# Attention followed by a bilinear feed-forward, on one core: the score products in another order, the side units of three batches placed anew, one product moved to GpSimd

## Chip, cores, metric

The kernel runs on one core of one Trainium2 chip. The metric is the device time of one execution in microseconds (us).

## The reference

Shapes: batch 8, heads 8, sequence 576, head size 64, 32 memory slots; feed-forward 512 to 1536 to 512.

```python
a = softmax(phi, axis=seq)                      # per memory slot
k_m = einsum('bhsm,bhsd->bhmd', a, k)           # 32 keys per head
v_m = einsum('bhsm,bhsd->bhmd', a, v)
attn = softmax(q @ k_m.T / sqrt(64))            # 576 x 32 per head
x = heads side by side of (attn @ v_m)          # 4608 x 512
out = ((x @ w_a) * (x @ w_b)) @ w_out
```

The kernel folds `v_m` into `w_a` and `w_b` ("vab"), so `x` is never made. For each batch it needs these *side units*:

- `exp`: exp of phi, on ACT.
- `kv`, `km`, `kvt`: sums of keys and values over the sequence (pkv), scaled copies of them (rep, VectorE), their transposes (pT, then kvT).
- `qt0` to `qt3`: transposes of q in 32x32 blocks (VectorE).
- `sc`, `e0`, `e1`: score products (pscore), exponentials E (ACT).
- `den`, `nr`: denominators (pD, then L = ln on ACT), R = exp(-L) on ACT, A = E x R, the *normalising product*.
- `v0` to `v2`, `x0` to `x2`: the fold (pva) and its copies from PSUM to vab, one on ACT and one on VectorE for each bank pair.

## The kernel before

Everything is placed by hand. The main loop emits *up* products of one batch (pa, pb: A times vab; ACT casts pa to a_sb, VectorE multiplies it with pb into ht) and after each step one slot of side units of the next batch; some products of the output stage (py, pv, px, with the ACT copy u and the output tile o_sb) fill up between them. GpSimd adds and subtracts parts of ht for that stage (h_sums) and issues the loads of later batches. In the slot strings below each word is one slot, `+` joins units and `-` leaves a slot empty.

```python
def scores(gs):
    ...
    for g in gs:                       # g: half of the heads
        t["pss", g] = [banks.take([P, NI, 32], F32, "pscore", hold=True) for _ in range(2)]
        for dh in range(2):            # the two halves of the contraction
            for z in range(2):
                for j in range(4):
                    r, hp = head(g, j)
                    row = 64 * r + 32 * z
                    nc.tensor.matmul(t["pss", g][z][0][32*j:32*j+32], kvT[row:row+32, ...], qTv[row:row+32, hp, ...],
                                     start=(dh == 0), stop=(dh == 1), tile_position=(row, 32 * j))
...
def normalise(g, hfs=slice(0, 2)):
    ...
    nc.scalar.activation(out=R, in_=L, func=AF.Exp, scale=-1.0)
    engine = nc.vector if b < 3 else nc.gpsimd
    engine.tensor_tensor(out=attn[b][:, g, sl], in0=E, in1=R, op=ALU.mult)
...
# inside the ups of batch 1 (second half): the units of batch 2
ups(half_steps(1, 1, 4), slots(2, "- kvt qt3 sc+e0+e1+den0 - nr0+den1+v0+x0a - - x0b+nr1 - v1+x1b x1a"))
# inside the ups of batch 2: the rest of batch 2, batch 3, and (with ') the start of batch 4
second = "v2_+x2a_+exp0 x2b_ exp1 - qt0+kv+km - qt1+qt2 kvt+qt3 sc+e0 - e1+v0+x0a ... - x2b+exp1' - qt0'+kv'+qt1' km' - qt2'+kvt'+qt3'"
```

The kernel hands out eight PSUM banks in turn: the next PSUM tile takes the bank that has been unused longest, so a matmul can wait for a bank that an ACT or VectorE copy has yet to read. In what follows a *tile* of TensorE is one 32x32 position; half `g` uses eight of the sixteen.

The softmax here doesn't subtract the row's maximum and nothing guards it: scores larger than these inputs give would overflow.

Of the kernel before, what the change touches and what calls it, by code (L numbers as in the profile page):

```python
# [18 lines left out]
def kernel(  # L19
# [11 lines left out]
    nc = tc.nc  # L31
# [60 lines left out]
    def load(b):  # L92
        load_phi(b)
        load_k(b)
        load_v(b)
        load_q(b)
# [84 lines left out]
    def head(g, j):  # L181

        jj = j ^ g
        return jj % 2, 2 * g + jj // 2

    def units(b):
# [91 lines left out]
        def scores(gs):  # L278
            if 0 in gs:
                t["E"] = mid.tile([P, 2, S], F16, name="E")  # L280
            if len(gs) > 1 and b > 2:
                work.settle()
            qTv = t["qT"].rearrange("p c (i s e) -> p c i e s", e=2, s=32)
            for g in gs:
                t["pss", g] = [banks.take([P, NI, 32], F32, "pscore", hold=True) for _ in range(2)]
                for dh in range(2):
                    for z in range(2):
                        for j in range(4):
                            r, hp = head(g, j)
                            row = 64 * r + 32 * z  # L290
                            nc.tensor.matmul(  # L291
                                t["pss", g][z][0][32 * j:32 * j + 32, :, :],
                                t["kvT"][row:row + 32, 2 * g + dh, M * j:M * j + M],
                                qTv[row:row + 32, hp, :, dh, :],
                                start=(dh == 0),
                                stop=(dh == 1),
                                tile_position=(row, 32 * j),
                            )
# [17 lines left out]
        def normalise(g, hfs=slice(0, 2)):  # L316
            if g == 0 and hfs.start == 0:
                attn[b] = mid.tile([P, 2, S], F16, name="A")
            sl = slice(HALF * hfs.start, HALF * hfs.stop)
            if hfs.start == 0:  # L320
                t["R", g] = small.tile([P, S], F16, name="R")
            nc.scalar.activation(out=t["R", g][:, sl], in_=t["L", g][:, sl], func=AF.Exp, scale=-1.0)  # L322
            engine = nc.vector if b < 3 else nc.gpsimd
            engine.tensor_tensor(out=attn[b][:, g, sl], in0=t["E"][:, g, sl], in1=t["R", g][:, sl], op=ALU.mult)  # L324

        def fold(lo, hi, zs):
# [27 lines left out]
        for z in range(2):  # L354
            u[f"exp{z}"] = one(exp_phi, z)
            u[f"ks{z}"] = one(sums, z, 0)
            u[f"kt{z}"] = one(transpose, z, 0)
            u[f"vs{z}"] = one(sums, z, 1)
            u[f"vt{z}"] = one(transpose, z, 1)
            u[f"s{z}"] = one(scores, (z,))  # L360
            u[f"e{z}"] = one(exp_scores, z)
            u[f"den{z}"] = one(denominators, z)
            u[f"nr{z}"] = one(normalise, z)
            for hf in range(2):
                u[f"nr{z}{hf}"] = one(normalise, z, slice(hf, hf + 1))
            for n in range(NCH):
                u[f"v{n}{'ab'[z]}"] = one(fold, 512 * n, 512 * (n + 1), (z,))
                u[f"x{n}{'ab'[z]}"] = one(take_fold, 512 * n, 512 * (n + 1), z)
            for n in range(2):
                u[f"hv{n}{'ab'[z]}"] = one(fold, 256 * n, 256 * (n + 1), (z,))  # L370
                u[f"hx{n}{'ab'[z]}"] = one(take_fold, 256 * n, 256 * (n + 1), z)
        for n in range(NCH):
            u[f"v{n}"] = one(fold, 512 * n, 512 * (n + 1), (0, 1))
        for x in range(4):
            u[f"qt{x}"] = one(q_transpose, x)
        u["sc"] = one(scores, (0, 1))
        u["kv"] = one(kv_sums)
        u["km"] = one(take_kv)
# [225 lines left out]
    def up(b, i, hfs):  # L604
        for hf in hfs:
            up_half(b, i, hf, 0)
        if len(hfs) > 1:
            yield
        for hf in hfs:
            up_half(b, i, hf, 1)  # L610
        yield

    def ups(steps, side=()):

        side = iter(side)
        for step in steps:
            for _ in up(*step):
                work.advance()
                next(side, us[step[0]]["-"])()
        for f in side:  # L620
            work.advance()
            f()
# [5 lines left out]
    def half_steps(b, hf, lo=0):  # L628

        return [(b, i, (hf,)) for i in range(lo, NFF)]  # L630
# [10 lines left out]
    def slots(b, names):  # L641

        def both(fs):
            return lambda: [f() for f in fs]
        def unit(n):
            if n == "fin":
                return lambda: work.pull(-work.done % NFF)
            if n == "L":
                return lambda: load(b + 2) if b + 2 < B else None
            if n[0] == "y":  # L650
                return lambda: some(int(n[1:]))
            if n[0] == "d" and n[1:].isdigit():
                return lambda: work.pull(int(n[1:]))
            return us[b + n.endswith("'") - n.endswith("_")][n.rstrip("'_")]

        return [both([unit(n) for n in x.split("+")]) for x in names.split()]
# [3 lines left out]
    def some(n):  # L660
        for _ in range(n):
            next(early, None)
# [24 lines left out]
    ups(steps(1, 0, 4), slots(1, "- hv1a+hx1a hv1b+hx1b+y1 - v1a+x1a y3+v1b x1b y3"))  # L687
    ups(half_steps(1, 0, 4), slots(1, "- v2a+x2a+v2b+x2b+qt0' - - qt1'+exp0'+qt2' exp1' - kv'+km'+y9"))
    work.plan(S + HALF, 10)
    ups(half_steps(1, 1, 4), slots(2, "- kvt qt3 sc+e0+e1+den0 - nr0+den1+v0+x0a - - x0b+nr1 - v1+x1b x1a"))  # L690
    second = "v2_+x2a_+exp0 x2b_ exp1 - qt0+kv+km - qt1+qt2 kvt+qt3 sc+e0 - e1+v0+x0a den0+x0b v1+x1a nr0+L x1b+exp0' den1 - nr1+v2+x2a - x2b+exp1' - qt0'+kv'+qt1' km' - qt2'+kvt'+qt3'"
    every = "- sc+e0 e1 den0 v0+x0a+x0b - - nr0+exp0' - - v1+x1a qt0' x1b+den1 exp1' - v2+x2a+x2b nr1+qt1' kv'+km' qt2' - qt3' - kvt'+L -"
    last = "sc+e0 - e1 - v0+x0b - x0a den1 - - den0 v1+x1b x1a+nr0 - - - - nr1+v2+x2a - - - - - x2b"
    for b in range(2, B):
# [37 lines left out]
```

## Time and profile before

| | before |
|---|---|
| median | 246.36 us (246.25 to 246.43) |
| TensorE busy | 233.6 us, 95% of a span of 244.6 us |
| VectorE, ACT, GpSimd busy | 69%, 64%, 63% |
| TensorE's three waits between 60 and 110 us | A 1.0, E 0.5, rep 0.4 us |
| idle TensorE from 105 to 203 us | none |

In the timelines each line is one merged run of alike instructions: start, length, engine, line, operation and, in brackets, how long the engine stood idle before it and what ended that. The prediction below shows the page's first line, the stages and the timelines. TensorE's waits of over 0.15 us between 60 and 203 us all stand where batches 2 and 4 are prepared. Its longest one, and the next up product after batch 2's last fold, from its timeline:

```profile
74.20 0.28 PE L591 MATMUL pa<-A,vab 128*128 128x288 f16 x1 [1.04 <-DVE A L324]
...
75.73 0.42 PE L591 MATMUL pa<-A,vab 128*128 128x288 f16 x2
```

### The profile page before, as it was taken

The numbers are of one execution on the slowest core, as the hardware profiler recorded it, in microseconds if no ns is written. First come the engines' busy times: TensorE is split into PE (matmuls) and PEld (weight loads), VectorE is DVE, ScalarE is ACT, GpSimd is POOL, SyncE is SP. The second block draws the span as 40 slices with busy tenths as digits, with TensorE's granted clock in tenths as the row PEclk, the third lists the DMA queues.
The fourth block names the chain that finished last, engine by engine and source line by source line (L and its number), as shares of the span: only waits on it lengthen the run. The fifth ranks groups of instructions, "written<-read, shape, count | busy, mean of one in ns | idle before, by whom it ended". The sixth has DMA issues, their size and how long they took to land.

```text
span 244.6 us, 7659 instructions
## 1 busy us (share of the span) xinstructions
PE 233.6 (95%) x3043; PEld 167.7 (69%) x3043; DVE 167.7 (69%) x403; ACT 157.2 (64%) x406; POOL 153.1 (63%) x128
## 2 busy tenths in 40 slices
PE   7979998999998999999999999999999999999993
PEld 2545654456666857767788777877787878888882
DVE  3536773568869868876994659865996576756642
ACT  2355761679697489578856768577856867565330
POOL 8722263499898029892899759892849177937001
PEclk9999999999999999999999999999999999999999
DMA  6999999999989704973159832696120403032154
GB/s 198 210 207 207 211 251 208 255 225 280 221 199 207 156 3 114 240 125 86 34 143 211 180 86 46 163 206 151 29 62 3 88 0 87 3 88 60 43 128 117
DMA packets 25044, 33.82 MB, mean 138 GB/s; under 512 B 1936, under 2 KB 19472, under 8 KB 25008
## 3 DMA queue, kind: packets, MB, share of 16 engines
q0 software_dynamic: 18288, 22.84, 50.3%
q1 hardware_dynamic: 6208, 9.70, 16.0%
q10 hardware_dynamic: 512, 0.79, 0.9%
q8 instruction: 24, 0.39, 0.7%
q14 instruction: 12, 0.10, 0.1%
HBM read 42.47 MB, written 9.44 MB: 212 GB/s over the span
## 4 chain that ended last, share of the span: by engine, by line
PE 77%; DMA 16%; DVE 3%; ACT 1%; issue 1%; POOL 0%; DVEq 0%
PE pa L591 18%; PE py L463 17%; PE pb L591 17%; PE pv L463 8%; DMA wo_sb<-in_moe_w_out_dram 7%; DMA wa_sb<-in_moe_w_a_dram 6%; PE pva L336 5%; PE px L463 4%; PE po L388 3%; DMA ht<-in_k_dram 2%; PE pkv L212 2%; PE pD L313 2%; PE pscore L291 1%; PE pT L241 1%; DVE A L324 1%
## 5 line engine op out<-in xcount | busy, mean ns | idle before, releaser
L602 DVE TENSOR_TENSOR ht<-a_sb,pb 128x288 f16<-128x288 f16 x168 | 73.1, 448 | 38.2 <-ACT a_sb L599 29.2
L591 PEld LDWEIGHTS <-vab 128*128 128x128 f16 x768 | 71.6, 98 | 28.2 <-issue 10.4
L599 ACT CAST a_sb<-pa 128x288 f16<-128x288 f32 x168 | 66.4, 406 | 28.0 <-PE pa L591 26.1
L591 PE MATMUL pa<-A,vab 128*128 128x288 f16 x384 | 75.8, 287 | 1.4 <-DVE A L324 1.0
L591 PE MATMUL pb<-A,vab 128*128 128x288 f16 x384 | 75.0, 286 | 0.3 <-ACT vab L348 0.3
L445 POOL TENSOR_TENSOR h_sums<-ht 128x768 f16<-128x768 f16 x28 | 45.9, 1641 | 37.8 <-DVE ht L602 37.3
L463 PEld LDWEIGHTS <-h_sums 128*128 128x128 f16 x384 | 37.4, 98 | 6.9 <-issue 0.4
L348 DVE CAST vab<-pva 128x512 f16<-128x512 f32 (+1 forms) x50 | 32.4, 663 | 3.3 <-PE pva L336 2.6
L348 ACT CAST vab<-pva 128x512 f16<-128x512 f32 (+1 forms) x50 | 27.9, 577 | 9.4 <-PE pva L336 9.3
L463 PEld LDWEIGHTS <-ht 128*128 128x128 f16 x288 | 28.2, 98 | 5.6 <-issue 0.4
L463 PE MATMUL py<-w_sums,h_sums 128*128 128x256 f16 x192 | 30.3, 272 | 0.0
L445 POOL TENSOR_TENSOR h_sums<-h_sums,ht 128x768 f16<-128x768 f16 x14 | 23.1, 1650 | 0.9
L445 POOL TENSOR_TENSOR h_sums<-ht,h_sums 128x768 f16<-128x768 f16 x14 | 23.0, 1643 | 1.0
L304 ACT ACTIVATE E<-pscore 128x288 f16<-128x288 f32 x32 | 11.4, 416 | 13.0 <-PE pscore L291 12.9
L324 POOL TENSOR_TENSOR A<-E,R 128x576 f16<-128x576 f16 x10 | 12.8, 1278 | 7.0 <-ACT R L322 6.8
L463 PE MATMUL py<-wo_sb,ht 128*128 128x256 f16 x96 | 16.0, 273 | 0.0
L463 PE MATMUL pv<-w_sums,h_sums 128*128 128x256 f16 x96 | 16.0, 272 | 0.0
L203 DVE STREAM_TRANSPOSE qT<-q_sb 128x288 f32<-128x288 f32 x32 | 14.3, 461 | 2.3 <-DMA q_sb<-in_q_dram 2.3
L470 ACT ACTIVATE u<-py 128x256 f32<-128x256 f32 x32 | 12.4, 388 | 5.2 <-PE py L463 4.9
L463 PE MATMUL py<-w_sums,ht 128*128 128x256 f16 x96 | 15.5, 272 | 0.1
L463 PE MATMUL px<-wo_sb,ht 128*128 128x256 f16 x96 | 15.4, 273 | 0.0
L314 ACT ACTIVATE L<-pD 128x288 f32<-128x288 f32 x32 | 11.5, 418 | 5.0 <-PE pD L313 4.7
(65 smaller groups left out, 274.0 us busy)
## 6 DMA issues: line engine op xcount, KB each, us to landing
out_dram<-o_sb SPq DMA_DIRECT2D x68, 128.0 KB, 2.4
kv_sb<-in_v_dram POOLq DMA_DIRECT2D x7, 576.0 KB, 10.4
phi_sb<-in_phi_dram POOLq DMA_DIRECT2D x7, 576.0 KB, 5.1
kv_sb<-in_k_dram POOLq DMA_DIRECT2D x7, 576.0 KB, 8.5
q_sb<-in_q_dram POOLq DMA_DIRECT2D x6, 576.0 KB, 13.1
wa_sb<-in_moe_w_a_dram POOLq DMA_DIRECT2D x3, 512.0 KB, 15.0
wb_sb<-in_moe_w_b_dram POOLq DMA_DIRECT2D x3, 512.0 KB, 16.2
wo_sb<-in_moe_w_out_dram POOLq DMA_DIRECT2D x3, 512.0 KB, 17.5
```

Source lines behind the costliest of these rows:

```text
L203: nc.vector.transpose(out=t["qT"][:, hp, :].bitcast(F32), in_=qs[b][:, hp, :].bitcast(F32))
L304: nc.scalar.activation(out=Ev[:, g, :, z, :], in_=pss, func=AF.Exp, scale=1.0 / (8.0 * CS))
L314: nc.scalar.activation(out=t["L", g][:, sl], in_=pD, func=AF.Ln)
L324: engine.tensor_tensor(out=attn[b][:, g, sl], in0=t["E"][:, g, sl], in1=t["R", g][:, sl], op=ALU.mult)
L336: nc.tensor.matmul(t["pva", lo, z][g][0][32 * j:32 * j + 32, 0:hi - lo], t["kvT"][64 * r:64 * r + 64, 4 + g, M * j:M * j + M], w_sbs[z][64 ...
L348: engine_copy(out=vabs[b][z][:, g, lo:hi], in_=pva[:, 0:hi - lo])
L445: engine.tensor_tensor(out=out, in0=in0, in1=in1, op=op)
L463: nc.tensor.matmul(po, lhs[:, i], rhs[:, i], start=first and i == 0, stop=i == KH - 1, skip_group_check=not first)
L470: nc.scalar.mul(out=x, in_=po, mul=scale)
L591: nc.tensor.matmul(ps, vabs[b][x][:, g, P * i:P * (i + 1)], attn[b][:, g, HALF * hf:HALF * (hf + 1)], start=(g == 0), stop=(g == 1))
L599: nc.scalar.copy(out=a_sbs[b, i, hf], in_=ps)
L602: nc.vector.tensor_tensor(out=ht[:, i, t0:t0 + HALF], in0=a_sbs.pop((b, i, hf)), in1=ps, op=ALU.mult)
```

## The change

Its intent: let sixteen different tiles follow one another in the score products, and take away TensorE's waits for E, A (batch 2) and rep (batch 4).

```diff
-            for g in gs:   # (banks taken here, unchanged)
-                for dh in range(2):
-                    for z in range(2):
+            for dh in range(2):
+                for z in range(2):
+                    for g in gs:
                         for j in range(4):
...
-            engine = nc.vector if b < 3 else nc.gpsimd
+            engine = nc.vector if b < 2 else nc.gpsimd
...
-    ... slots(2, "- kvt qt3 sc+e0+e1+den0 - nr0+den1+v0+x0a - - x0b+nr1 - v1+x1b x1a"))
+    ... slots(2, "- kvt qt3 sc+e0+e1 - den0+den1 nr0+nr1 v0+x0a x0b - v1+x1b x1a"))
-    second = "... - qt0+kv+km - qt1+qt2 kvt+qt3 sc+e0 - e1+v0+x0a ... - qt0'+kv'+qt1' km' - qt2'+kvt'+qt3'"
+    second = "... - kv+km qt0 qt1 kvt qt2+qt3 sc+e0 e1+v0+x0a ... - kv'+km' qt0'+qt1' - qt2'+kvt'+qt3'"
```

More of the change, by code (lines that the diff above doesn't have):

```diff
@@ L689 @@
     work.plan(S + HALF, 10)
-    ups(half_steps(1, 1, 4), slots(2, "- kvt qt3 sc+e0+e1+den0 - nr0+den1+v0+x0a - - x0b+nr1 - v1+x1b x1a"))
-    second = "v2_+x2a_+exp0 x2b_ exp1 - qt0+kv+km - qt1+qt2 kvt+qt3 sc+e0 - e1+v0+x0a den0+x0b v1+x1a nr0+L x1b+exp0' den1 - nr1+v2+x2a - x2b+exp1' - qt0'+kv'+qt1' km' - qt2'+kvt'+qt3'"
+    ups(half_steps(1, 1, 4), slots(2, "- kvt qt3 sc+e0+e1 - den0+den1 nr0+nr1 v0+x0a x0b - v1+x1b x1a"))
+    second = "v2_+x2a_+exp0 x2b_ exp1 - kv+km qt0 qt1 kvt qt2+qt3 sc+e0 e1+v0+x0a den0+x0b v1+x1a nr0+L x1b+exp0' den1 - nr1+v2+x2a - x2b+exp1' - kv'+km' qt0'+qt1' - qt2'+kvt'+qt3'"
     every = "- sc+e0 e1 den0 v0+x0a+x0b - - nr0+exp0' - - v1+x1a qt0' x1b+den1 exp1' - v2+x2a+x2b nr1+qt1' kv'+km' qt2' - qt3' - kvt'+L -"
```

## The prediction

> **What bounds the kernel now.** I read the page first, then busy time by stage, then what TensorE waits for, then the timelines around those waits.
>
> ```profile
> PE 233.6 (95%) x3043; PEld 167.7 (69%) x3043; DVE 167.7 (69%) x403; ACT 157.2 (64%) x406; POOL 153.1 (63%) x128
> ```
>
> TensorE has 95% of the span, no other engine over 69%. Busy time by stage (columns: stretch, length, then busy us of PE, PEld, DVE, ACT, POOL, with clock and DMA) says where the missing 5% lies.
>
> ```profile
> 65.98:76.00 10.02, 8.43 (x125) 5.03 (x125) 7.24 (x15) 8.77 (x25) 9.84 (x9) 1.00 0.97 203
> 76.00:98.00 22.00, 21.92 (x311) 16.15 (x309) 17.69 (x44) 17.36 (x46) 10.52 (x9) 1.00 0.54 110
> 98.00:105.20 7.20, 6.84 (x151) 4.87 (x150) 6.28 (x19) 3.71 (x11) 6.31 (x5) 1.00 1.18 235
> 105.20:203.00 97.80, 97.80 (x1253) 75.19 (x1250) 72.29 (x171) 72.21 (x191) 69.70 (x49) 1.00 0.48 101
> ```
>
> From 105 to 203 us TensorE is never idle: there only less TensorE work can help. Before that, two stretches lose 1.59 and 0.36 us; these hold batches 2 and 4's side units, and TensorE's waits from 60 to 110 us are just three:
>
> ```profile
> PE pa L591 <- DVE A L324: 1.0, 1, 1.0
> PE pD L313 <- ACT E L304: 0.5, 1, 0.5
> PE pT L241 <- DVE rep L232: 0.4, 1, 0.4
> ```
>
> The change aims at all three. Timelines of batch 2 (start us, duration us, engine, line, instruction) show the first wait's origin:
>
> ```profile
> 69.64 0.46 DVE L324 TENSOR_TENSOR A<-E,R 128x576 f16<-128x576 f16 x1
> ...
> 72.70 1.45 DVE L324 TENSOR_TENSOR A<-E,R 128x576 f16<-128x576 f16 x1
> ```
> ```profile
> 72.17 1.65 POOL L445 TENSOR_TENSOR h_sums<-ht 128x768 f16<-128x768 f16 x1
> ```
>
> The same product took 0.46 us while GpSimd issued transfers, and 1.45 us when it started inside a GpSimd sum.
>
> **What the Trainium skill says.** "SBUF — State Buffer", section "Who interferes with whom": a VectorE instruction with two SBUF inputs and a GpSimd one that reads SBUF exclude each other; the later is blocked whole. The trace agrees: the sum ended at 72.17 + 1.65 = 73.82, and the product ended at 74.15. "GPSIMD Engine Reference", section 4.1: two-input elementwise work is about twice as slow on GpSimd. Here it is 1.278 us (group of ten) against 0.46, 2.8 times. "TensorEngine Tiling (Array Packing)", Key Properties: different tiles work in parallel, and a change of tiling mode drains the array. The trace agrees with both: going from 128x128 to 32x32 costs 94 ns over the ordinary spacing (last start before a score block 159.459 us, 256 columns of about 109 ns, first score start 159.662). "TensorE: Matmul & The Clock Gate", Part 3, The mechanism: matmuls start in strict program order. The trace disagrees: in batch 5's score block the second visit to the first eight tiles starts at 159.803, after the first visit to the other eight (159.715), although the program has it earlier.
>
> **The change part by part.**
>
> 1. *Score order.* One block is 32 matmuls of 32x32x288. A tile's second visit starts 0.141 us after its first (159.662 to 159.803), starts within a group are about 3.3 ns apart. Before: eight tiles, the same eight, the other eight twice; since the chip already lets the other eight overtake, the last start was 159.879, 0.217 us after the first. After: 16 x 3.3 = 53 ns for the first visits, and the last second visit starts at 0.141 + 0.053 = 0.194 us. That is 23 ns per block, not half of it. What follows is fixed: last start to the next matmul takes 0.215 us (159.879 to 160.094). Batches 0 and 1 make scores for one half alone, so nothing moves there. Batches 2 and 4 wait for other data (below). Left are batches 3, 5, 6, 7: 4 x 23 = **0.1 us**.
>
> 2. *Batch 2: product to GpSimd, the denominators two slots later, both normalisations together.* TensorE's stalls here: the wait for E (0.55 idle), the wait for A (1.04), and bank waits. I worked ACT through, for it runs without a gap from 66.47 to 73.91. Pitches from this trace: E 0.295 us, L 0.29, R 0.59, a_sb 0.35, vab 0.47, u 0.28. The first E starts some 0.15 later than before (66.62), as it now shares the wait for the last q transpose (matmul start 66.243) with the rest. Then 4 E, 2 a_sb, 4 L, a_sb, u put R at 70.3 and 70.9, ending at 71.0 and 71.6. GpSimd has ended its fourth sum at 69.2, so A is made 71.04 to 72.3 and 72.3 to **73.5**; before it was ready at 74.15. The other chain to the same matmul is a_sb (to 71.9), ht on VectorE (to 72.3), the copy of the first fold (to 72.95), which frees the bank that the v1 fold waits for; TensorE then starts batch 2's up products at 73.62 and the half that needs the second A at 73.74. It was 74.197. The v2 fold, held by the v1 copies (TensorE's 0.2 us there becomes about the same), passes at 75.33 where the next up product was at 75.735. The stalls for E and A, 1.6 us together, so give back only **0.4 us**, because ACT has the same work to do between them: TensorE arrives early and waits for banks instead. GpSimd's 2 x 1.28 = 2.56 us delay the loads of batch 4 and the next sums; before, the sums ended at 78.97 and the first was used at 83.7; after, they start near 76.5, the first ends at 78.2, the last at 83.1, needed near 89. Hidden.
>
> 3. *Batch 3's units.* The score block moves one slot later, its exponentials' second half and the v0 fold come right after. The fold's second half finds its bank held by an a_sb that ACT takes between the exponentials: about 0.3 us of wait, as now (the block v0 took 87.298 to 88.172, 0.874, where an undisturbed one takes 0.557), plus 0.1 at the next up product and 0.07 at a bank of the k-v sums. **-0.15 us**.
>
> 4. *Batch 4's units.* km now comes before the q transposes, so rep is done before 101.8 and the 0.8 us that the six pT transposes lose (0.36 idle, the rest hidden in weight loads) goes. But VectorE is full here:
>
> ```profile
> 102.10 0.74 DVE L232 TENSOR_SCALAR rep<-pkv,rphi 128x256 f16<-128x256 f32 x2
> 102.77 0.44 DVE L602 TENSOR_TENSOR ht<-a_sb,pb 128x288 f16<-128x288 f16 x1
> 103.13 0.47 DVE L203 STREAM_TRANSPOSE qT<-q_sb 128x288 f32<-128x288 f32 x1
> 103.52 0.52 DVE L242 COPY kvT<-pT 128x768 f16<-128x768 f16 x1
> 103.96 0.46 DVE L203 STREAM_TRANSPOSE qT<-q_sb 128x288 f32<-128x288 f32 x1
> 104.34 0.41 DVE L602 TENSOR_TENSOR ht<-a_sb,pb 128x288 f16<-128x288 f16 x1
> ```
>
> It runs from 99.17 to 105.5 without a gap, and the score block's last eight first visits began at 104.812, just after that last ht (104.76) freed their bank. The built program of the changed kernel has the same set of VectorE work ahead of that ht, in another order. So the score block waits where pT waited: **0 us** of its own.
>
> Sum: 0.1 + 0.4 - 0.15 + 0 = 0.35 us. TensorE's full stretch to 203 us carries the gain to the end, where the last waits (0.2 us) follow ht of the last batch and move along. 246.36 - 0.35 = **246.0 us**.
>
> **The rivals.** *All stalls vanish.* If the waits for E, A and rep go and nothing takes their place, 0.55 + 1.04 + 0.8 is 2.4 us, and with the score order some 2.5: 243.9. For it speaks that TensorE is the bound and these are its only waits; against it the gapless ACT and VectorE stretches. *The tile order halves a score block.* Two visits of 0.12 us streaming would be 0.24 instead of four; at 0.22 us for each of six blocks, 1.3 us: 244.7. Against it, the overtaking seen in the trace. *GpSimd comes in the way.* Two products of 1.28 us in a row end later than the VectorE one would: if R comes 0.7 us later than I have it (one more wait for a bank ahead of an L), A is ready at 74.2 and the gain of part 2 is gone; with batch 3's loss the time is 246.4 or 246.5. *No change*: every stall only moves, 246.3.
>
> **Range and chances.** Part 2 decides: it is between 0 and about 1.2 us (1.6 less what remains of bank waits), with 0.4 most likely; part 4 between 0 and 0.5, if VectorE's order lets its last ht finish earlier; part 3 between -0.3 and +0.2. Together 245.2 to 246.6. A change of over 2% would be 4.9 us, twice what all stalls hold, and for a slowdown nothing of that size is in sight: 1% each way.
>
> **What would show it.** In the changed profile: score blocks in batches 5 to 7 have the last start about 0.19 us after the first and the next up product about 23 ns earlier than 0.43; A on GpSimd twelve times at 1.28, the second of batch 2 ending near 73.5; batch 2's first up product near 73.6, waiting for a bank or for A; the pT transposes of batch 4 without a wait, but a score block near 104.3 that stands until ht; from 105 to 203 a full TensorE. I am wrong if ACT has idle time between 66.6 and 72 us (then part 2 is smaller), if the E and A waits go and no bank wait follows (then it is larger), or if the q transposes of batch 3 or 4 wait for late loads.

## The result

The changed kernel takes 245.59 us (245.41 to 245.71, four runs), the kernel before 246.31 us (246.20 to 246.43) in the same rounds. The ratio is 0.997, interval 0.9953 to 0.9988. It is a real gain of about 0.7 us, far within 2%.

The page of the changed kernel, and its busy time by stage, with the columns as before:

```profile
PE 234.6 (96%) x3043; PEld 168.1 (69%) x3043; DVE 166.2 (68%) x401; ACT 157.2 (64%) x406; POOL 155.6 (64%) x130
```
```profile
65.98:76.00 10.02, 9.38 (x130) 5.68 (x130) 5.89 (x13) 9.26 (x25) 8.17 (x8) 1.00 0.46 93
76.00:98.00 22.00, 21.92 (x310) 16.18 (x308) 17.70 (x43) 17.38 (x46) 15.05 (x13) 1.00 0.80 163
98.00:105.20 7.20, 6.97 (x151) 5.09 (x149) 6.16 (x18) 3.76 (x11) 6.47 (x5) 1.00 1.18 232
105.20:203.00 97.80, 97.80 (x1251) 75.12 (x1250) 72.25 (x171) 72.24 (x191) 69.78 (x50) 1.00 0.48 101
```

In batch 2's stretch TensorE is busy 0.95 us longer, but gets through only five more matmuls, so "busy" overstates the gain. A matmul's record is equally long whether the next one is held or not (those of the v1 fold take 0.37 to 0.39 us, and without a hold the next starts 3 ns after), and only idle time beyond its end counts as waiting. A hold of up to that length hides behind the record. ACT is now busy 9.26 of 10.02 us. What TensorE waits for between 60 and 110 us:

```profile
PE pD L314 <- DVE ht L603: 0.2, 1, 0.2
PE pva L337 <- DVE vab L349: 0.2, 1, 0.2
```

All three waits of before are gone; two bank waits stand in their place. The timeline of TensorE in batch 2 shows them, and one that the list does not name, inside the group at 71.90 (its first matmul starts at 71.897 and its second only at 72.385, which leaves 0.12 us of idle time, too little for the list):

```profile
68.86 0.28 PE L314 MATMUL pD<-E,ones 128*128 128x288 f16 x1 [0.20 <-DVE ht L603]
...
71.90 0.90 PE L337 MATMUL pva<-wa_sb,kvT 64*32 64x512 f16 x8
72.41 0.39 PE L337 MATMUL pva<-wb_sb,kvT 64*32 64x512 f16 x1
72.99 0.41 PE L337 MATMUL pva<-wb_sb,kvT 64*32 64x512 f16 x7 [0.19 <-DVE vab L349]
73.33 0.39 PE L464 MATMUL pv<-wo_sb,h_sums 128*128 128x256 f16 x2
73.55 0.41 PE L592 MATMUL pa<-A,vab 128*128 128x288 f16 x2
...
75.16 0.42 PE L592 MATMUL pa<-A,vab 128*128 128x288 f16 x2
```

The v1 fold (71.90 to 73.33, 1.43 us) takes 0.87 us longer than the v0 fold just before it (70.49 to 71.05, 0.56 us): it waits for banks that ht and the fold copies have yet to read. The second A (GpSimd's timeline) is ready at 71.07 + 2.51 = 73.58, just before TensorE comes to the half that needs it (73.676):

```profile
71.07 2.51 POOL L325 TENSOR_TENSOR A<-E,R 128x576 f16<-128x576 f16 x2 [1.81 <-ACT R L323]
```

**Reading parts inside a trace.** The start-up, up to batch 2's score block, is the same program in all thirteen kernels, yet the block starts at 65.52 to 66.54 us in their profiles. So I take that start as zero and compare where the same matmul stands later: the up product after batch 2's v2 fold (before: 75.735 - 65.982 = 9.75 us), the one after batch 3's v1 fold (24.58), the one after batch 4's scores (39.20), and the last matmul of the third px group from the end (163.82). The table gives the difference to the kernel before, negative when earlier, one profile each.

| run | after v2 fold, batch 2 | after v1 fold, batch 3 | after scores, batch 4 | near the end |
|---|---|---|---|---|
| changed kernel | -0.61 | -0.52 | -0.58 | -0.62 |
| order_only | +0.19 | +0.20 | +0.20 | +0.12 |
| old_order | -0.82 | -0.73 | -0.79 | -0.76 |
| product_vector | -0.53 | -0.44 | -0.50 | -0.58 |
| old_slots2 | -0.12 | -0.03 | -0.09 | -0.13 |
| old_slots34 | -0.60 | -0.60 | -0.59 | -0.64 |
| q_early | -0.61 | -0.52 | -1.30 | -1.35 |
| casts_vector | -1.05 | -0.97 | -1.03 | -1.10 |
| best | -0.23 | -0.15 | -0.93 | -1.01 |
| best2 | -1.07 | -0.99 | -1.77 | -1.85 |
| best3 | -1.60 | -1.52 | -2.30 | -2.38 |
| best4 | -0.42 | -0.33 | -1.11 | -1.19 |

What a stage gains stays to the end, because TensorE is full from 105 to 203 us. How far one profile can be trusted, the rows show themselves: the changed kernel, q_early and old_slots34 are the same program up to the first point and stand at -0.607, -0.608 and -0.603 there.

### The profile page after: what moved, and what is told of

Same layout as the page of the kernel before. It is cut to its first block, busy times and chain, and to the rows that moved or that the text cites. A ratio compares the mean times of both kernels' runs of the same rounds, so it can differ in the third digit from the quotient of the medians. Undisturbed runs are those within 1.5% of the kernel's fastest.

```text
span 244.0 us, 7661 instructions
## 1 busy us (share of the span) xinstructions
PE 234.6 (96%) x3043; PEld 168.1 (69%) x3043; DVE 166.2 (68%) x401; ACT 157.2 (64%) x406; POOL 155.6 (64%) x130
## 4 chain that ended last, share of the span: by engine, by line
PE 76%; DMA 16%; DVE 3%; ACT 2%; issue 1%; POOL 0%; DVEq 0%
PE pa L592 17%; PE py L464 17%; PE pb L592 16%; PE pv L464 8%; DMA wo_sb<-in_moe_w_out_dram 7%; DMA wa_sb<-in_moe_w_a_dram 6%; PE pva L337 5%; PE px L464 4%; PE po L389 3%; DMA ht<-in_k_dram 2%; PE pkv L212 2%; PE pscore L292 1%; PE pD L314 1%; PE pT L241 1%; ACT E L305 1%
## 5 line engine op out<-in xcount | busy, mean ns | idle before, releaser
L325 POOL TENSOR_TENSOR A<-E,R 128x576 f16<-128x576 f16 x12 | 15.3, 1278 | 8.8 <-ACT R L323 8.6
L194 ACT ACTIVATE exp_sb<-phi_sb 128x576 f16<-128x576 f32 x16 | 11.0, 698 | 5.3 <-DMA phi_sb<-in_phi_dram 5.3
```

The lines of the kernel that those rows point to most:

```text
L194: nc.scalar.activation(out=t["exp"][:, 2 * z:2 * z + 2, :, :], in_=phis[b][:, 2 * z:2 * z + 2, :].rearrange("p c (i m) -> p c i m", m=M), ...
L325: engine.tensor_tensor(out=attn[b][:, g, sl], in0=t["E"][:, g, sl], in1=t["R", g][:, sl], op=ALU.mult)
```

## The experiments

My theory: the order saves only nanoseconds, batch 2 gains by its placement as far as ACT's chain and the banks allow, batch 4 gains almost nothing because VectorE's queue is full. The rivals: the order is the gain; the engine of the product is the gain; a removed wait is worth its length. All runs below gave correct results; each kernel had four to six timed runs, against 11 or 12 of the kernel before. The changed kernel was not run again; the others are compared with its four runs above and with its trace.

### order_only: the order alone

```diff
 # kernel before
-            for g in gs:
-                for dh in range(2):
-                    for z in range(2):
+            for dh in range(2):
+                for z in range(2):
+                    for g in gs:
```

> The kernel before with the new order of the score products and nothing else. Theory (the chip lets other tiles overtake, so the order saves only the 23 ns between the last starts of batches 3, 5, 6, 7; batches 2 and 4 wait for data): 0.07 to 0.12 us faster than before, about 246.2. Rival (the order halves each of six score blocks): 1.3 us faster, about 245.0. In the trace: last score start 0.19 us after the first, against 0.217.

Measured: 246.39 us, ratio 1.0004 (0.9992 to 1.0016). The rival's 1.3 us is excluded. The trace shows that my sum was wrong in sign: TensorE loses 0.19 us in batch 2 and wins back 0.08 us by the end. ACT's timelines show why, first the kernel before, then this one (the score block starts at 65.98 and 66.03):

```profile
66.47 1.32 ACT L304 ACTIVATE E<-pscore 128x288 f16<-128x288 f32 x4
```
```profile
66.73 1.01 ACT L305 ACTIVATE E<-pscore 128x288 f16<-128x288 f32 x3 [0.32 <-PE pscore L292]
```

In batch 2 the last q transpose comes after the block has begun. Before, half 0 did not need it and its E could start 0.49 us after the block's start (66.47 - 65.98). In the new order a matmul that needs it is the seventh of 32, so that none of the four score banks is complete before it in the program, and E starts 0.70 us after (66.73 - 66.03). In the undisturbed blocks the gain is as small as I had it: in batch 6 the single records give 0.190 us from first to last start in the changed kernel, 0.217 before.

```profile
159.66 0.50 PE L291 MATMUL pscore<-qT,kvT 32*32 32x288 f16 x32
160.09 0.42 PE L591 MATMUL pa<-A,vab 128*128 128x288 f16 x2
```
```profile
159.08 0.47 PE L292 MATMUL pscore<-qT,kvT 32*32 32x288 f16 x32
159.49 0.42 PE L592 MATMUL pa<-A,vab 128*128 128x288 f16 x2
```

From block to next product: 0.43 before (first fence), 0.41 in the changed kernel (second).

### old_order: everything but the order

```diff
 # changed kernel
-            for dh in range(2):
-                for z in range(2):
-                    for g in gs:
+            for g in gs:
+                for dh in range(2):
+                    for z in range(2):
```

> The changed kernel with the score products in the order of before. Theory: 0.05 to 0.12 us slower than the changed kernel, about 245.7. Rival (the order carries the gain): the whole 0.7 us goes, 246.3.

Measured: 245.46 us, ratio 0.9967 (0.9955 to 0.9979), against 0.997 for the changed kernel; the times cannot tell the two apart. The traces can: without the new order TensorE leaves batch 2 another 0.21 us earlier (-0.82 against -0.61) and is 0.13 us ahead near the end. My expectation had the sign wrong, and the rival is out: the gain stays without the new order. The new order is a small loss in this kernel.

### product_vector: batch 2's product back on VectorE

```diff
 # changed kernel
-            engine = nc.vector if b < 2 else nc.gpsimd
+            engine = nc.vector if b < 3 else nc.gpsimd
```

> The changed kernel with batch 2's normalising products back on VectorE, units placed as in the changed kernel. Theory (what counts is that the products no longer start inside a GpSimd sum, and that ACT's chain sets R; with the new placement R is ready near 70.9 and 71.5 us while GpSimd only issues loads, until about 72.2): both products take about 0.46 us, and the time is within 0.2 us of the changed kernel. Rival (GpSimd is what takes the product out of the way; on VectorE it takes 1.45 us and holds TensorE as before): 0.6 to 0.9 us slower than the changed kernel.

Measured: 245.63 us, ratio 0.9978 (0.9966 to 0.999), within the 0.2 us expected. (The profile is of the longest run, 246.37 us, whose score block starts 0.5 us later than the changed kernel's.) TensorE leaves batch 2 at -0.53 instead of -0.61. VectorE's and GpSimd's timelines of this run:

```profile
71.55 1.02 DVE L325 TENSOR_TENSOR A<-E,R 128x576 f16<-128x576 f16 x2 [0.40 <-ACT R L323]
72.48 0.45 DVE L603 TENSOR_TENSOR ht<-a_sb,pb 128x288 f16<-128x288 f16 x1
```
```profile
71.97 0.75 POOL L90 DMA_DIRECT2D q_sb<-in_q_dram  x1
73.02 1.64 POOL L446 TENSOR_TENSOR h_sums<-ht 128x768 f16<-128x768 f16 x1 [0.30 <-DVE ht L603]
```

Two products take 1.02 us together, not 1.45 us for one, since GpSimd only issues loads until 72.7. So GpSimd is not what saves the product here: the new placement moves it out of the sum's way on either engine. What GpSimd adds is some 0.08 us, which fits ht: with the products ahead of it in VectorE's queue it starts 5.94 us after the block's start (72.48 - 66.54) instead of 5.87 (71.88 - 66.01).

### old_slots2: batch 2's units as before, product on GpSimd

```diff
 # changed kernel
-"- kvt qt3 sc+e0+e1 - den0+den1 nr0+nr1 v0+x0a x0b - v1+x1b x1a"
+"- kvt qt3 sc+e0+e1+den0 - nr0+den1+v0+x0a - - x0b+nr1 - v1+x1b x1a"
```

> The changed kernel with batch 2's units placed as before (denominators at once after the scores, normalisations apart), product on GpSimd. Theory: the 0.55 us wait for E is back, the second R ends near 72.7 again, GpSimd makes the second A to about 74.0, so TensorE's first up product of batch 2 is about 0.3 us later than in the changed kernel: 245.9. Rival (the engine of the product is all that counts): same as the changed kernel, 245.6. Rival (the placement is all): 246.2 to 246.3.

Measured: 246.05 us, ratio 0.9991 (0.9978 to 1.0004), between the rivals, and 0.46 us above the changed kernel where I had expected 0.3. TensorE's waits between 60 and 110 us in this run:

```profile
PE pa L592 <- POOL A L325: 0.9, 1, 0.9
PE pD L314 <- ACT E L305: 0.7, 1, 0.7
```

The wait for E is back, and longer than before the change (0.7 against 0.5), which fits the new order's 0.2. With order_only at +0.19 and this run at -0.12, moving the product alone is worth 0.30 us where units stand as before. Going from this run to the changed kernel, -0.12 to -0.61, placement is worth 0.49 us. The trace shows where the 0.30 us come from: the half that needs the second A starts 8.295 us after the block's start, in order_only 8.401, and the v2 fold is no longer held for 0.19 us by VectorE's copies, ahead of which the product had stood.

With product_vector, all four combinations have been run (all with the new order): placement is worth 0.72 us with the product on VectorE (+0.19 to -0.53). It is a bundle, though: denominators later, normalisations together, folds after both. No run separates these moves.

### old_slots34: the units of batches 3 and 4 as before

```diff
 # changed kernel
-second = "... - kv+km qt0 qt1 kvt qt2+qt3 sc+e0 e1+v0+x0a ... - kv'+km' qt0'+qt1' - qt2'+kvt'+qt3'"
+second = "... - qt0+kv+km - qt1+qt2 kvt+qt3 sc+e0 - e1+v0+x0a ... - qt0'+kv'+qt1' km' - qt2'+kvt'+qt3'"
```

> The changed kernel with the units of batches 3 and 4 placed as before. Theory (batch 3's new placement costs about 0.08 us, batch 4's removes the pT wait but TensorE meets VectorE's queue again at the score block and keeps 0.06): within 0.1 us of the changed kernel, the pT waits of 0.8 us back in the trace. Rival (the removed pT wait is worth its length): 0.6 to 0.8 us slower than the changed kernel.

Measured: 245.62 us, ratio 0.9971 (0.9957 to 0.9985), equal to the changed kernel; after batch 4's scores -0.59 against -0.58. The wait for rep is back, and costs 0.06 us: across batch 4 TensorE gains nothing here (-0.595 to -0.594), where the changed kernel gains 0.06 (-0.523 to -0.582). Batch 3's new placement had cost about 0.07 (-0.523 against -0.595), so the two cancel. The wait:

```profile
PE pT L241 <- DVE rep L232: 0.4, 1, 0.4
```

In the changed kernel the same time is lost inside the score block. Its TensorE and VectorE timelines there:

```profile
103.54 1.15 PE L292 MATMUL pscore<-qT,kvT 32*32 32x288 f16 x32
104.63 0.42 PE L592 MATMUL pa<-A,vab 128*128 128x288 f16 x2
```
```profile
103.41 0.46 DVE L203 STREAM_TRANSPOSE qT<-q_sb 128x288 f32<-128x288 f32 x1
103.79 0.42 DVE L603 TENSOR_TENSOR ht<-a_sb,pb 128x288 f16<-128x288 f16 x1
```

From the block to the next product it takes 1.09 us (103.54 to 104.63) instead of 0.41, and no list of waits names this. The single records show two holds: after six starts, until 103.921 (the last q transpose ends at 103.87), and after six more, until 104.260 (ht ends at 104.21). Each record lasts 0.28 to 0.30 us, so the holds, of 0.36 and 0.32 us, leave idle gaps of only 0.07 and 0.03 us, and the rest counts as busy.

### q_early: two q transposes out of VectorE's full stretch

```diff
 # changed kernel, end of second
-den1 - nr1+v2+x2a - x2b+exp1' - kv'+km' qt0'+qt1' - qt2'+kvt'+qt3'
+den1 qt0' nr1+v2+x2a qt1' x2b+exp1' - kv'+km' - - qt2'+kvt'+qt3'
```

> The changed kernel with two of batch 4's q transposes taken out of VectorE's full stretch (99 to 105 us) and put into the two empty slots before it. Theory (batch 4's score block waits for nothing but VectorE's queue there): the block starts without the extra 0.2 us and takes 0.41 instead of 1.09 us, the time is 0.6 to 0.9 us lower than the changed kernel's: 244.8. Rival (something else holds the block: loads, banks of ACT, or the order of tiles): within 0.15 us of the changed kernel.

Measured: 245.18 us, ratio 0.9952 (0.9937 to 0.9966). In the trace the whole gain lies in the score block of batch 4, as expected: -0.52 before it as in the changed kernel, -1.30 after it. (The times show 0.4 of these 0.8 us; their intervals allow both.) The block on TensorE's timeline:

```profile
103.11 0.63 PE L292 MATMUL pscore<-qT,kvT 32*32 32x288 f16 x32
103.68 0.42 PE L592 MATMUL pa<-A,vab 128*128 128x288 f16 x2
```

It still takes 0.57 rather than the 0.41 us that I had expected, but it starts without a wait; the 0.16 us left are a hold from 103.149 to 103.311, and ht ends at 103.26. So VectorE's queue was what held batch 4, which old_slots34 alone could not show.

### casts_vector: four casts from ACT to VectorE

```diff
 # changed kernel
-            nc.scalar.copy(out=a_sbs[b, i, hf], in_=ps)
+            (nc.vector.tensor_copy if b == 1 and hf == 1 and i >= 8 else nc.scalar.copy)(out=a_sbs[b, i, hf], in_=ps)
```

> The changed kernel with the four casts of a_sb in the last four up products of batch 1 taken from ACT and given to VectorE, which idles 1 to 1.8 us at a time there. Theory (ACT's chain of E, a_sb, L, u, R sets when A and the banks are ready): R ends about 1.2 us earlier, the second A near 72.6, the waits of the denominators' products and of the v1 fold shrink, TensorE leaves the v2 fold of batch 2 0.8 to 1.1 us earlier than in the changed kernel: 244.7. Rival (the bank waits are VectorE's own chain of ht and fold copies, which gets longer): same as the changed kernel or up to 0.5 us slower.

Measured: 245.14 us, ratio 0.9951 (0.9936 to 0.9966); batch 2 left at -1.05, so 0.44 us gained over the changed kernel, half of what I expected. TensorE's longest wait is now for A (0.7 us), and ACT's timeline says why A came no earlier:

```profile
68.29 1.32 ACT L315 ACTIVATE L<-pD 128x288 f32<-128x288 f32 x4 [0.28 <-PE pD L314]
69.76 0.38 ACT L471 ACTIVATE u<-pv 128x256 f32<-128x256 f32 x1 [0.15 <-PE pv L464]
70.04 1.25 ACT L323 ACTIVATE R<-L 128x576 f16<-128x576 f32 x2
```

R starts at 70.04 against 70.19 in the changed kernel: ACT, relieved of four casts (some 0.35 us each), waits for TensorE's pD and for u's pv instead. So "ACT's chain sets A" was only partly right. The casts held the banks, and that part went; R also hangs on u, which stands ahead of it in ACT's queue although R does not need it.

### best, best2, best3, best4: towards a faster version

`best` is q_early and casts_vector together, with the old score order in batch 2 alone and batch 2's product on VectorE:

```diff
+            for outer in ([(0,), (1,)] if len(gs) > 1 and b == 2 else [gs]):   # dh, z, g in outer, j inside
...
+            engine = nc.vector if b < 3 else nc.gpsimd
```

> A version meant to beat both: the changed kernel with q_early and casts_vector together, batch 2's product on VectorE, and batch 2's score products in the old order (one half's four heads complete first, so the first E does not wait for the last q transpose). Theory: the parts add, -0.7 for q_early, -0.9 for casts_vector, -0.2 for the order, and with the earlier R up to -0.4 for the faster product: 243.3 to 243.9. Rival (the chains run into one another, so parts do not add): 244.3 to 244.8.

Measured: 245.14 us, ratio 0.9951 (0.9937 to 0.9964). A miss, outside both expectations: batch 2 is left at only -0.23. VectorE now has the casts, and the two products stand ahead of the last cast in its queue, where VectorE first stands idle for 0.75 us until R is there:

```profile
PE pva L338 <- DVE a_sb L601: 0.6, 1, 0.6
```

`best2` puts the product back on GpSimd (`b < 2`).

> The version of before (best) with batch 2's product back on GpSimd: early q transposes, casts on VectorE, old score order in batch 2. Theory (in best the two products stood in VectorE's queue ahead of the last cast of a_sb and so of the banks; without that the parts add): -0.76 for the q transposes, -0.44 for the casts and about -0.2 for the order against the changed kernel, 244.2. Rival (the early q transposes take something from the casts' gain, or the order's 0.2 is eaten by the wait for A): 244.5 to 244.8.

Measured: 244.33 us, ratio 0.9918 (0.9904 to 0.9932). The q transposes (-0.78, from -0.99 to -1.77) and the casts add up. The order's 0.2 us does not show: batch 2 is left at -1.07 against casts_vector's -1.05, as the wait for A takes it up (in the single records the half that needs the second A comes 0.84 us late in both). So GpSimd for the product is right once VectorE is loaded: next to `best` it is worth 0.84 us.

`best3` puts `nr0+nr1` into the slot of `den0+den1`, ahead of u:

```diff
-"- kvt qt3 sc+e0+e1 - den0+den1 nr0+nr1 v0+x0a x0b - v1+x1b x1a"
+"- kvt qt3 sc+e0+e1 - den0+den1+nr0+nr1 - v0+x0a x0b - v1+x1b x1a"
```

> best2 with batch 2's normalisations in the slot of the denominators, so ACT makes both R straight after the four L instead of after u, which waits for TensorE. Theory (with casts on VectorE, TensorE's last wait is for A behind R): R starts 0.4 us earlier, the wait for A of about 0.7 us falls to 0.2 to 0.4, time 0.3 to 0.5 us below best2. Rival (what follows on ACT, u and the fold copies, then holds the banks): same as best2 within 0.15 us.

Measured: **243.66 us** (243.57 to 243.72), ratio 0.9892 (0.9877 to 0.9907), below best2 by 0.67 us in the medians and 0.53 in the traces, a little more than expected. The wait for A falls to 0.2 us. This version beats both kernels: 2.6 us under the kernel before, where the change had brought 0.7.

```profile
PE pa L593 <- POOL A L326: 0.2, 1, 0.2
```

`best4` makes the first product on VectorE and the second on GpSimd (`nc.vector if b < 2 or (b == 2 and g == 0) else nc.gpsimd`).

> best3 with batch 2's first product on VectorE and the second on GpSimd. Theory: the second A is ready another 0.6 us earlier, but the first product stands for about 0.5 us in VectorE's queue ahead of a cast and a fold copy: within 0.3 us of best3 either way. Rival (A is the only wait left): 0.3 to 0.6 us below best3.

Measured: 244.93 us, ratio 0.994 (0.9925 to 0.9955), 1.27 us slower than best3, outside both expectations. The first product in VectorE's queue costs far more than its own length: batch 2 is left 1.18 us later (-0.42 against -1.60), with waits for a_sb and ht on VectorE where there had been one for A. VectorE's timeline shows where the delay begins:

```profile
70.08 0.46 DVE L326 TENSOR_TENSOR A<-E,R 128x576 f16<-128x576 f16 x1 [1.16 <-ACT R L324]
70.45 0.45 DVE L601 CAST a_sb<-pa 128x288 f16<-128x288 f32 x1
```

The product stands next in the queue, and VectorE is idle for 1.16 us until R is there. The third cast, behind it, starts at 70.45; in best3 it starts at 68.81. I have not traced the later steps.

## Why the prediction was right, point by point

The measured 245.59 us lies in the range of 245.2 to 246.6, and the class (within 2%) was right. The gain was 0.72 us in the medians and 0.62 us in the traces against a predicted 0.35: the mechanisms held, one had the wrong sign in total, and one term was too small. These two errors pull in opposite directions, so that the total came as close as it did is in part luck; and a range of 1.4 us that also holds "no change" (246.3) says little by being met. What supports the account are its steps:

1. *Score order.* The 23 ns per undisturbed block held (27 ns between first and last start in batch 6; the sum had counted 16 steps of 3.3 ns where there are 15, and 0.141 + 0.050 gives 0.191 against 0.190 us measured). What failed is treating this part as a gain: in batch 2 the order makes the first E wait for the last q transpose, which I had seen and put at 0.15 us inside part 2; the runs show 0.19 to 0.21. Order as a whole costs about 0.13 us, as order_only and old_order both show.
2. *Batch 2.* Predicted 0.4, measured 0.61 us with the order's loss in it, and 0.82 without (old_order). The chain of steps came out close: A ready at 73.58 (predicted 73.5), the up products from 73.55 (73.62), the next up product at 75.16 (75.33). Counted from the block's start (66.01 against 65.98), the last is 0.20 us earlier than predicted. Half of this was there at the first up product. The other half is the v2 fold: I had allowed 1.59 us from the half that needs the second A to the next up product (1.54 before), and it took 1.48, as the hold inside the fold fell from 0.19 to 0.13 us. That the E and A waits would turn into bank waits held. That the sum had held the product is borne out by product_vector, where each product, made while GpSimd only issues loads, takes 0.458 us. That the product was blocked *whole* is not: before, it ended 0.33 us after the sum, which is less than 0.46. How placement and engine share the gain I had not worked out; it depends on the order in which they are taken (0.30 for the engine with old placement, 0.08 with the new).
3. *Batch 3.* Predicted a loss of 0.15, measured 0.08.
4. *Batch 4.* Predicted 0, measured a gain of 0.06, and old_slots34 and q_early confirm the reason: the pT wait moves into the score block. Two readings were loose. Before, only four of the first visits waited for the last ht, not eight (twelve of the sixteen start by 104.762). And the rest of the 0.8 us was not hidden in weight loads, which stood idle for 0.50 us at that point, but behind the ends of the pT records.
5. *GpSimd's load.* The delayed loads and sums stayed hidden, as said; from 76 to 98 us TensorE is busy 21.92 us in both kernels. None of the three signs of being wrong came up: ACT stays busy from 66.71 on, bank waits follow, and no q transpose waits for a load.

The rivals "all stalls vanish" (243.9) and "the order halves a block" (244.7) fell with the result. Two of the prediction's figures do not add up: 1.3 us less than 246.36 is 245.06, not 244.7, and its parts' best cases add to 2.0 us, so to 244.4 and not to the 245.2 given.

## What to carry to other kernels

In this kernel a wait that the profile named on the bound engine was worth its length only where the queue behind it had room: work through the next in-order queue (here ACT in batch 2, VectorE in batch 4) to the following point where the engine meets it. Moving work *out of* a full stretch (two transposes, four casts) paid 0.4 to 0.8 us each. Reordering *within* one paid 0.06 in batch 4, where the same VectorE work stayed ahead of the instruction that TensorE waited for, and 0.5 to 0.7 us where it took something out of the way of such an instruction (batch 2's placement; R ahead of u in best3). An instruction that itself waits also holds what stands behind it in its queue (best4). And look inside groups of matmuls: holds of some 0.3 us hide behind their records, and no list of waits shows them.

## What the Trainium skill lacked or had wrong

- "TensorE: Matmul & The Clock Gate", Part 3, The mechanism, says that matmuls start in strict program order. Here those of one group of 32x32 tiles began while earlier ones of other tiles were still held: in the kernel before, batch 6, the second visit to the first eight tiles starts at 159.803, later than the first visit to the other eight at 159.715, though the program has it earlier. (The records' semaphore marks agree: the waits for the other half's banks come before the first of the four marks that release E, while in the program the first half's two marks come first.) (The prediction calls this block batch 5's by mistake; with batches counted from 0 it is batch 6's.) So sixteen tiles in a row save 27 ns of 217, not half a block.
- "TensorEngine Tiling (Array Packing)", Key Properties, says that a change of tiling mode drains the array, without a size. Here the change from 128x128 to 32x32 tiles adds 94 ns (159.459 to 159.662, less some 109 ns of ordinary spacing), and 0.215 us pass from the last 32x32x288 start to the next full-size one, where two full-size products of 288 columns start 0.123 us apart.
- "GPSIMD Engine Reference", section 4.1, has two-input elementwise work about twice as slow as on VectorE; for 128x576 in fp16 it is 1.278 against 0.46 us here, 2.8 times.
- No page says how long a hold between matmuls can be before a profile shows it. Here the records of 32x32x288 products are 0.28 to 0.30 us long, held or not, so that in the changed kernel batch 4's score block, with holds of 0.36 and 0.32 us inside, counts as 1.15 us of work where an undisturbed one counts 0.47.
